# Column-group products in every second step from 20 to 30, full-array transposes of exponentials, and weight loads spread and issued ahead of the far writes

## The chip, the cores and the metric

The kernel runs on one core of a Trainium2 chip. The metric is the device time of one execution in microseconds; the median of the runs counts. The engines are TensorE (PE), VectorE (DVE), ScalarE (ACT) and GpSimd (POOL); SyncE (SP) issues the transfers. Each engine works through its own instructions in program order and waits on semaphores for the others.

## The reference

Three stages follow one another on the same tokens (4 batches, 8 heads, 576 positions, head size 64: 2304 tokens of 512 numbers). The first is causal attention with a decay. The other two, with names shortened:

```python
# stage 2: dense layer, 512 -> 2048 -> 512
h = x @ w_in
g = h * (1 / (1 + exp(-h)))
x = g @ w_out
# stage 3: soft mixture of 8 experts with 4 slots each (32 slots)
logits = x @ phi
d = softmax of logits over the tokens          # for each slot
slot_input = d.T @ x                           # 32 x 512, by experts
slot_out = relu(slot_input @ w1) @ w2          # each expert its own w1, w2
c = softmax of logits over the slots           # for each token
return c @ slot_out
```

## The kernel before

Attention takes the first 200 us or so, then the weights of stage 2 are prepared. Stage 2 and the sums of stage 3 run in 36 **steps**, numbered k from 0 to 35. Each belongs to a chunk c of 256 tokens (nine chunks, 0 to 8) and a group fg of 512 hidden numbers (four groups). From step 16 on a chunk's four groups follow one another: step 16 is (4,0), step 20 (5,0), step 24 (6,0), step 28 (7,0). A step has 24 products `h` (L594 to L596; two halves t of 128 tokens, 12 products each, f32 split into parts), and each half ends in ScalarE's tanh (`g_tanh`, L608) and VectorE's product (`g_mul`, L615), which give `gt`: tokens on partitions.

The work of stage 3 is put between the steps. Because the logits are linear, stage 2's second product is not made for each token: `W'` (`WP`, w_out times phi) turns g straight into logits. That needs g with hidden numbers on partitions, `gr`. There are two ways from gt to gr:
- `g_tr`, locally: eight transposes on TensorE over the full array (`gtp`, L658) and two copies on ScalarE (L659) into a buffer of the pool `w0` with the tag "t", which has two buffers;
- the "far" way: `blocks` has VectorE transpose blocks of 32 (`gb`, L667) and writes them to the chip's memory (`far`, L670), and `placed` reads them back in four transfers (`gr<-far`, L676). Before step 25 gb lies in a page of its own; from step 25 on (`own` false) it lies in a buffer of tag "t", as g_tr's result does.

`g_lp` then makes the logits of one (c,fg): products into four column groups of 32 columns (`lp`, L685), four side by side. When a chunk has its four groups, `chunk_soft` takes its logits (`sl`, L774) to exponentials, `chunk_w` transposes these (`etp`, L801) and makes the weights of both softmaxes, and `chunk_acc` adds the chunk's share to the slot sums (`pp`, L825, column groups again; accumulated by VectorE, L832). lp, pp and etp are not full-array products of 128 columns; h, gtp and sl are.

The order is written by hand in the functions at the end: after the h products of step k, `stacked(k)` does what is due of lp and pp and calls `place(k)`, which reads far tiles back; `square(k)` does transposes (g_tr by `turn_next`, chunk_w) and `turn_far`, which sends new far tiles out; `halfway(k)` stands between the two halves of a step. A list `flying` holds the (c,fg) that are on their way to g_lp.

The expert weights w1, w2 and the prepared w_out come in **units** of 512 KB (`load_unit`, L442, L448, L450) into free pages; `ROOM` says how many units may have been asked for by which step. All these transfers are issued by SyncE, in program order, in one queue.

Of the kernel before, what the change touches and what calls it, by code (L numbers as in the profile page):

```python
# [24 lines left out]
NPAGES = 25  # L25
NW = 8
STEPS = (17, 25, 30)
RATE = 1.5
CAPS = ((0, 12), (5, 6))
LAG = 1  # L30
ROOM = ((18, 5), (20, 6), (21, 7), (22, 10), (24, 11), (25, 12), (26, 17), (28, 19), (30, 23), (32, 29), (33, 32), (34, 35), (35, 42), (36, 45))
PARTS = ((0, 256, {}), (256, 128, {0: 1, 3: 2, 5: 2, 7: 2}), (384, 128, {1: 3, 3: 2, 5: 2, 7: 1}))
RING_A, RING_B, RING_T = "014", "235", "b"

# [2 lines left out]
def tile_attention_moe_softmoe(ctx: ExitStack, tc: tile.TileContext, qk, vr, f, wcat, phi, w1, w2, out):  # L37
    nc = tc.nc
# [6 lines left out]
    NCH = 9  # L45
# [13 lines left out]
    mo = {}  # L59

    def bank(ring, shape, name):
        tags = RINGS[ring]
        turn[ring] += 1
        ch = tags[turn[ring] % len(tags)]
        return ps.tile(shape, F32, name=name, tag=("av" if ch in "ab" else "b") + ch, bufs=1)

    ident = keep.tile([128, 128], F32, name="ident")
# [356 lines left out]
    def page(shape, name, dtype=F32):  # L424
        sl = FREE.pop(0)
        return sl[0].tile(shape, dtype, name=name, tag=sl[1], bufs=1), sl
# [293 lines left out]
    sm = {}  # L720

    def arena(a, **parts):
        at = 0
        for name, shape in parts.items():
            n = int(np.prod(shape))
            v = a[:, at:at + n]
            sm[name] = v.rearrange("p (a b) -> p a b", b=shape[1]) if len(shape) == 2 else v
            at += n
        assert at <= a.shape[1]
# [10 lines left out]
        arena(page([128, 1024], "arena")[0], WP=(2 * 8, 32), acc=(512,))  # L740

    def arena_b():
        arena(page([128, 1024], "arena")[0], sel=(128,), phi=(4, 32), wt=(2, 32), cw=(2 * NCH, 32), selz=(32,),
              mc=(1,), cm=(2, 1), cs=(2, 1), nm0=(1,), nm1=(1,), zc=(1,), sc0=(1,), sc1=(1,), z=(1,))
        nc.sync.dma_start(out=sm["phi"], in_=phi)
        for j in range(4):
            nc.vector.tensor_copy(sm["sel"][:, 32 * j:32 * j + 32], sm["rep"])
# [44 lines left out]
        scale()  # L792

    def chunk_w(c):
        e, wt, z, cm = sm["e"], sm["wt"], sm["z"], sm["cm"]
        cw = sm["cw"][:, 2 * c:2 * c + 2]
        tp = bank("g", [128, 2, 64], "etp")
        last = c == NCH - 1
        for t in range(2):
            n = 32 if last else 64  # L800
            nc.tensor.transpose(tp[:, t, 0:n], e[0:n, 128 * t:128 * t + 128], ident[0:n, 0:n])  # L801
        nc.vector.tensor_copy(wt, tp[:, :, 0:32])
        if c == 0:
            nc.vector.tensor_copy(z, sm["zc"])
        else:
            nc.vector.scalar_tensor_tensor(z, z, sm[f"scale{c}"], sm["zc"], op0=ALU.mult, op1=ALU.add)

        def weights():
            if last:
                for t in range(2):  # L810
                    nc.tensor.transpose(tp[:, t, 32:64], sm["ls"][32:64, 128 * t:128 * t + 128], ident[32:64, 32:64])
            tl = tp[:, :, 32:64]
            nc.vector.tensor_reduce(cm, tl, axis=AX.X, op=ALU.max)
            nc.vector.tensor_tensor(cw, tl, cm.to_broadcast([128, 2, 32]), ALU.subtract)
            nc.scalar.activation(cw, cw, AF.Exp)

        sm["weights"] = weights

    def chunk_acc(c):
        acc = sm["acc"]  # L820
        pp = bank("g", [128, 512], "pp")
        gt = [GT.pop((c, j)) for j in range(4)]
        for t in range(2):
            for j in range(4):
                nc.tensor.matmul(pp[32 * j:32 * j + 32], lhsT=sm["wt"][:, t], rhs=gt[j][:, t], start=(t == 0),  # L825
                                 stop=(t == 1))
        if c == 0:
            nc.vector.tensor_copy(acc, pp)
        else:
            n = 512 if c < NCH - 1 else 256  # L830
            for x in range(0, 512, n):
                nc.vector.scalar_tensor_tensor(acc[:, x:x + n], acc[:, x:x + n], sm[f"scale{c}"], pp[:, x:x + n],  # L832
                                               op0=ALU.mult, op1=ALU.add)
        release(*(GS.pop((c, j)) for j in range(4)))
# [197 lines left out]
    with tc.manual_schedule():  # L1032
# [66 lines left out]
            return 2 * fg + 1 in made and (c < 2 or c - 2 in read)  # L1099

        def turn_next(k):
            for f in rows[:3]:
                if turns[0] and born.get(f, 99) < int(k) and ready(*f) and f not in FAR:
                    turns[0] -= 1
                    turns[1] = k
                    rows.remove(f)
                    flying.append((k, *f))
                    g_tr(*f)
                    return
# [16 lines left out]
        def place(k):  # L1126
# [3 lines left out]
            for f in list(rows):  # L1130
                if f in FAR and born[f] < k and f[0] - rows[0][0] < 2 and ready(*f) and turns[0]:
# [2 lines left out]
                    flying.append((k, *f))  # L1134
                    placed(*f)

        def turn_soft():
            if soft:
                chunk_soft(soft[0])
                exps.append(soft.pop(0))  # L1140
                if soft:
                    chunk_ls(soft[0])

        def halfway(k):
            if STEPS[0] < k < STEPS[2]:
                turn_next(k - 0.5)
            turn_soft()

        def stacked(k):
            for f in sorted(flying, key=lambda f: f[1:]):  # L1150
                c, fg = f[1:]
                if f[0] < k:
                    flying.remove(f)
                    g_lp(c, fg)
                if SUMMED.get(c) == 4 and f not in flying:
                    if not soft:
                        chunk_ls(c)
                    soft.append(c)
            place(k)
            if acc and acc[0][0] < k:  # L1160
                chunk_acc(acc.pop(0)[1])
            if stage[0] is not None:
                w_prime_b(stage[0])

        def square(k):
            if stage[1] is not None:
                w_prime_c(stage[1])
            stage[1], was = stage[0], len(rows)
            stage[0] = mo["wp"].pop(0)[1] if mo["wp"] and mo["wp"][0][0] < k - bool(CQ) else None
            if stage[0] is not None:  # L1170
                w_prime_a(stage[0])
            else:
                turn_next(k)
            if exps:
                chunk_w(exps[0])
                chunk_cw(exps[0])
                acc.append((k, exps.pop(0)))
            turn_next(k)
            if k >= (NCH - 1) * 4:
                turn_soft()  # L1180
            if stage[0] is None and not STEPS[0] <= k < STEPS[2]:
                turn_next(k)
            turn_far(k)
            if stage[1] is not None and len(rows) < was:
                w_prime_c(stage[1])
                stage[1] = None

        conv_ops(OPS)
        for k, (c, fg) in enumerate(steps):
# [61 lines left out]
            elif fg != 2:  # L1251
                stacked(k + 0.5)
                if fg == 1:
                    square(k + 0.5)
            mo["umax"] = max([0] + [n for at, n in ROOM if k + 1 >= at])
            pump()
        assert not (soft or exps or acc) and rows == [(NCH - 1, 3)] and not mo["wp"], (soft, exps, acc, rows, mo["wp"])
        end()
        tail()
# [53 lines left out]
```

## Time and profile before

| | us |
|---|---|
| median of three runs | 536.07 (534.09 to 536.73) |
| profiled execution | 534.51 |
| its span, first to last instruction | 532.8 |
| TensorE busy (matmuls) | 506.1, 95% |
| TensorE loading weights, beside the matmuls | 373.7, 70% |
| VectorE busy | 338.1, 63% |
| ScalarE busy | 295.9, 56% |
| GpSimd busy | 212.8, 40% |

The span is what the profile covers; the execution's time is 1.7 us longer. In the rows a product's own duration overlaps with that of the next, since matmuls are pipelined: what a product costs is read from its start to the start of the next row. `x16` in a row joins 16 records that followed one another; each lp of one (c,fg) has eight records, a pp sixteen. In the stretch 310 to 444, which holds most of the changed steps, TensorE is busy 130.17 of 134 us. The granted clock of TensorE is 0.995 of full speed over the span.

The h products of step k end, and what stands behind them begins, at: step 22 at 359.28 us, 23 at 367.61, 24 at 375.08, 25 at 384.88, 27 at 403.58.

### The profile page before, as it was taken

How to read it: one execution, taken by the hardware profiler on the slowest of the kernel's cores; microseconds unless marked ns; L12 is line 12 of the kernel's file. 1: busy time of each engine (PE TensorE's matmuls, PEld its weight loads, DVE VectorE, ACT ScalarE, POOL GpSimd, SP SyncE). 2: the span in 40 equal slices, each digit the busy share in tenths (PEclk: the TensorE clock that was granted, in tenths of full speed). 3: DMA queues.
4: the chain of work that ended last, by engine and by line, in shares of the span. 5: the costliest groups of instructions: out<-in, count | busy, mean ns of one | idle time of the engine just before them, and what ended most of it. 6: DMA issues, size and time to landing. Idle time of an engine off the chain costs nothing.

```text
span 532.8 us, 11447 instructions
## 1 busy us (share of the span) xinstructions
PE 506.1 (95%) x4219; PEld 373.7 (70%) x4219; DVE 338.1 (63%) x896; ACT 295.9 (56%) x587; POOL 212.8 (40%) x237
## 2 busy tenths in 40 slices
PE   8899999999999999899999999999998999999994
PEld 4687887787777787587777777667675667674563
DVE  6766777677788389999989633655654431435033
ACT  8798889888886676557646554223421333331022
POOL 9777788888887304447466300000000000013000
PEclk9999999999999999999999999999999999999998
DMA  5727755665653387212431109699698818668998
GB/s 145 225 68 209 199 167 173 177 194 156 147 174 88 111 334 277 111 41 79 159 119 61 59 27 329 198 262 275 219 340 213 282 51 338 246 234 337 409 405 304
DMA packets 44108, 105.81 MB, mean 199 GB/s; under 512 B 8180, under 2 KB 17172, under 8 KB 44052
## 3 DMA queue, kind: packets, MB, share of 16 engines
q1 hardware_dynamic: 44052, 105.08, 60.3%
q8 instruction: 33, 0.54, 0.4%
q14 instruction: 23, 0.19, 0.1%
HBM read 82.58 MB, written 17.52 MB: 188 GB/s over the span
## 4 chain that ended last, share of the span: by engine, by line
PE 61%; DMA 12%; DVE 10%; ACT 7%; POOL 4%; issue 3%; SPq 2%; DVEq 0%; POOLq 0%; ACTq 0%
PE h L594 8%; PE h L596 8%; PE h L595 8%; PE av L304 4%; PE st L247 3%; PE gtp L658 3%; PE mx L201 3%; PE rs L288 3%; PE st L249 3%; PE lp L685 3%; PE so L959 3%; DMA gr<-far 3%; PE h L897 3%; DMA QA<-mr 3%; DMA far<-gb 2%
## 5 line engine op out<-in xcount | busy, mean ns | idle before, releaser
L594 PE MATMUL h<-w,xh 128*128 128x512 f32 x280 | 115.4, 412 | 3.7 <-DVE gt L615 3.7
L596 PE MATMUL h<-w,xh 128*128 128x512 f32 x280 | 110.5, 395 | 0.0
L595 PE MATMUL h<-w,xl 128*128 128x512 f32 x280 | 110.2, 394 | 0.0
L615 DVE SCALAR_TENSOR_TENSOR gt<-gt,h 128x512 f32<-128x512 f32 x70 | 46.9, 681 | 59.9 <-ACT gt L608 59.7
L608 ACT ACTIVATE gt<-h 128x512 f32<-128x512 f32 x70 | 41.4, 594 | 77.6 <-PE h L596 65.7
L253 ACT ACTIVATE E<-st 128x256 f32<-128x256 f32 (+4 forms) x160 | 63.5, 432 | 12.7 <-PE st L249 9.8
L207 DVE CUSTOM_DVE_ANT_0 junk<-mx,mask 128x64 bf16<-128x64 f32 (+3 forms) x128 | 50.0, 414 | 31.6 <-PE mx L201 30.8
L757 POOL COPY arena<-arena 128x128 f32<-128x128 f32 x4 | 1.1, 294 | 171.7 <-ACT gt L608 156.7
L594 PEld LDWEIGHTS h<-w,xh 128*128 128x128 f32 x280 | 52.6, 188 | 20.5 <-DVE gt L615 6.4
L596 PEld LDWEIGHTS h<-w,xh 128*128 128x128 f32 x280 | 52.6, 188 | 12.4
L247 PE MATMUL st<-QA,KA 128*128 128x256 f32 (+2 forms) x192 | 55.4, 300 | 5.3 <-DMA QA<-mr 2.9
L595 PEld LDWEIGHTS h<-w,xl 128*128 128x128 f32 x280 | 52.7, 188 | 10.7
L201 PE MATMUL mx<-KA,QA 127*128 127x64 f32 (+2 forms) x192 | 50.1, 327 | 2.0 <-DVE mr L222 1.0
L249 PE MATMUL st<-QB,KB 128*128 128x256 f32 (+2 forms) x192 | 51.6, 294 | 0.0
L270 POOL TENSOR_SCALAR_AFFINE_SELECT E<-E 128x256 f32<-128x256 f32 (+1 forms) x96 | 41.1, 444 | 26.1 <-ACT E L253 25.0
L304 PE MATMUL av<-E,VF 128*64 128x320 f32 (+4 forms) x448 | 50.8, 364 | 0.0
L179 POOL TENSOR_TENSOR QB<-qk,QA 64x576 fp32r<-64x576 f32 x30 | 42.8, 1428 | 2.3
L177 POOL TENSOR_TENSOR KB<-qk,KB 64x576 fp32r<-64x576 f32 x30 | 42.4, 1434 | 1.7 <-ACT KB L171 0.6
L304 PEld LDWEIGHTS av<-E,VF 128*64 128x64 f32 x448 | 29.5, 136 | 17.8 <-POOL E L270 0.3
L524 POOL TENSOR_TENSOR raw<-raw 128x512 f32<-128x512 f32 x16 | 26.9, 1681 | 37.1 <-ACT raw L513 30.0
L247 PEld LDWEIGHTS st<-QA,KA 128*128 128x128 f32 x192 | 34.6, 180 | 9.7 <-ACT E L253 7.1
L201 PEld LDWEIGHTS mx<-KA,QA 127*128 127x128 f32 x192 | 32.8, 189 | 6.1 <-DVE Mt L207 1.7
(170 smaller groups left out, 881.1 us busy)
## 6 DMA issues: line engine op xcount, KB each, us to landing
unit<-in_w_dram SPq DMA_DIRECT2D x64, 512.0 KB
raw<-in_w_dram SPq DMA_DIRECT2D x32, 512.0 KB
far<-gb SPq DMA_DIRECT2D x16, 512.0 KB
gr<-far SPq DMA_DIRECT2D x64, 128.0 KB
qk<-in_qk_dram SPq DMA_DIRECT2D x14, 576.0 KB
VF<-in_v_dram SPq DMA_DIRECT2D x16, 320.0 KB
RB<-R SPq DMA_DIRECT2D x32, 144.0 KB
WO<-wt SPq DMA_DIRECT2D x8, 512.0 KB
```

Of the source, the lines that this page charges most:

```text
L177: eng.tensor_tensor(KB.of(p)[0:64, h], src[64:128], KB.of(p)[64:128, h], ALU.subtract)
L179: eng.tensor_tensor(QB.of(p)[64:128, h], src[0:64], QA[p % 3][0:64, h, 64:640], ALU.subtract)
L201: nc.tensor.matmul(t[:, 0:w], lhsT=qa[0:127, h, 128 * blk:128 * blk + 128], rhs=ka[0:127, h, k0:k0 + w], start=True, stop=True)
L207: nc.vector.tensor_tensor_reduce(out=junk[:, 0:w], in0=t[:, 0:w], in1=mask[:, 448 - w:448], scale=1.0, scalar=Mx[p][:, h] if j == 5 else - ...
L247: nc.tensor.matmul(t[0:m, o:o + n], lhsT=ka[:, h, k0:k0 + m], rhs=qa[:, h, 64 + q0:64 + q1], start=True, stop=False)
L249: nc.tensor.matmul(t[0:m, o:o + n], lhsT=kb_[:, h, k0:k0 + m], rhs=qb[:, h, q0:q1], start=False, stop=True)
L253: nc.scalar.activation(e[0:m], t[0:m, 0:o], AF.Exp, scale=0.125)
L304: nc.tensor.matmul(AVP[p][x][64 * h:64 * h + 64, o0:o0 + n], lhsT=VF[p % 2][:, kb, h], rhs=E[2 * p + h][kb][:, c:c + n], start=kb == 0, st ...
L594: nc.tensor.matmul(o, lhsT=xh[:, d, tok], rhs=w[:, 0], start=(d == 0), stop=False)
L595: nc.tensor.matmul(o, lhsT=xl[:, d, tok], rhs=w[:, 0], start=False, stop=False)
L596: nc.tensor.matmul(o, lhsT=xh[:, d, tok], rhs=w[:, 1], start=False, stop=(d == 3))
L615: nc.vector.scalar_tensor_tensor(g, g, 1.0, h[:, n * j:n * j + n], op0=ALU.add, op1=ALU.mult)
```

## The change

Six things are changed in the steps 17 to 31:
- in the even steps of `APART` `stacked` only reads far tiles back; their lp and pp are made in the next odd step, together with that step's own;
- the transposes of exponentials (`etp`) take the full array: 128 rows instead of 64 (32 for the last chunk), into a buffer twice as wide;
- `wt`, the transposed exponentials, has two places, so that two chunks can stand side by side, since pp of one chunk may now come after the etp of the next;
- `turn_next` turns nothing locally in step 26 and while two local results are waiting;
- the units that a step loads (`rooms`) are issued within `square`, ahead of `turn_far`, in steps 17 to 30; before, they came at the end of the step, behind it;
- `ROOM` spreads the units over the steps: before, five at step 17, 1, 1, 3, 1, 1, 5, 2, 4 at steps 19, 20, 21, 23, 24, 25, 27, 29 and 6 at step 31; now 1, 2, 2, 3, 3, 3, 2, 3, 2 at steps 18, 21, 23, 25, 26, 27, 28, 29, 30 and 8 at step 31. By the end of step 31 both have 29.

```diff
+APART = (20, 22, 24, 26, 28, 30)
+ALONE = (26,)
...
-ROOM = ((18, 5), (20, 6), (21, 7), (22, 10), (24, 11), (25, 12), (26, 17), (28, 19), (30, 23), (32, 29), (33, 32), (34, 35), (35, 42), (36, 45))
+ROOM = ((19, 1), (22, 3), (24, 5), (26, 8), (27, 11), (28, 14), (29, 16), (30, 19), (31, 21), (32, 29), (33, 32), (34, 35), (35, 42), (36, 45))
...
     def arena_b():
-        arena(page([128, 1024], "arena")[0], sel=(128,), phi=(4, 32), wt=(2, 32), cw=(2 * NCH, 32), selz=(32,),
+        arena(page([128, 1024], "arena")[0], sel=(128,), phi=(4, 32), wt=(4, 32), cw=(2 * NCH, 32), selz=(32,),
               mc=(1,), cm=(2, 1), cs=(2, 1), nm0=(1,), nm1=(1,), zc=(1,), sc0=(1,), sc1=(1,), z=(1,))
+        sm["wt"] = sm["wt"].rearrange("p (c t) s -> p c t s", c=2)
...
     def chunk_w(c):
-        e, wt, z, cm = sm["e"], sm["wt"], sm["z"], sm["cm"]
+        e, wt, z, cm = sm["e"], sm["wt"][:, c % 2], sm["z"], sm["cm"]
         cw = sm["cw"][:, 2 * c:2 * c + 2]
-        tp = bank("g", [128, 2, 64], "etp")
         last = c == NCH - 1
+        tp = bank("g", [128, 4, 128], "etp")
         for t in range(2):
-            n = 32 if last else 64
-            nc.tensor.transpose(tp[:, t, 0:n], e[0:n, 128 * t:128 * t + 128], ident[0:n, 0:n])
-        nc.vector.tensor_copy(wt, tp[:, :, 0:32])
+            nc.tensor.transpose(tp[:, t], e[:, 128 * t:128 * t + 128], ident)
+        nc.vector.tensor_copy(wt, tp[:, 0:2, 0:32])
...
                 for t in range(2):
-                    nc.tensor.transpose(tp[:, t, 32:64], sm["ls"][32:64, 128 * t:128 * t + 128], ident[32:64, 32:64])
-            tl = tp[:, :, 32:64]
+                    nc.tensor.transpose(tp[:, 2 + t], sm["ls"][:, 128 * t:128 * t + 128], ident)
+            tl = tp[:, 2 * last:2 * last + 2, 32:64]
...
@@ -822,7 +824,7 @@
         gt = [GT.pop((c, j)) for j in range(4)]
         for t in range(2):
             for j in range(4):
-                nc.tensor.matmul(pp[32 * j:32 * j + 32], lhsT=sm["wt"][:, t], rhs=gt[j][:, t], start=(t == 0),
+                nc.tensor.matmul(pp[32 * j:32 * j + 32], lhsT=sm["wt"][:, c % 2, t], rhs=gt[j][:, t], start=(t == 0),
...
         def turn_next(k):
+            if k in ALONE or sum(f[1:] not in GRS for f in flying) == 2:
+                return
...
+        def rooms(k):
+            mo["umax"] = max([0] + [n for at, n in ROOM if k + 1 >= at])
+            pump()
...
+        def chunk_exps(k):
+            if exps:
+                chunk_w(exps[0])
+                chunk_cw(exps[0])
+                acc.append((k, exps.pop(0)))
+
         def stacked(k):
+            if k in APART:
+                place(k)
+                return
+            if k - 1 in APART:
+                chunk_exps(k - 0.5)
+                if len(acc) > 1:
+                    chunk_acc(acc.pop(0)[1])
...
-            if exps:
-                chunk_w(exps[0])
-                chunk_cw(exps[0])
-                acc.append((k, exps.pop(0)))
+            chunk_exps(k)
             turn_next(k)
...
+            if STEPS[0] <= k < 31:
+                rooms(k)
             turn_far(k)
...
-            mo["umax"] = max([0] + [n for at, n in ROOM if k + 1 >= at])
-            pump()
+            rooms(k)
```

**Where it moves instructions: TensorE.** Line numbers of the changed kernel are two or three higher. The rows are the work between the h products (left out at "..."), from the end of step 24 to the end of step 26 in the kernel before (lp and pp of step 24, lp and pp of step 25, sl, then step 26):

```order
L685 MATMUL lp<-gr,arena 32x256 x8
L825 MATMUL pp<-gt,arena 32x512 x8
L658 MATMUL gtp<-ident,gt 128x128 x8
L801 MATMUL etp<-ident,small 128x64 x2
...
L685 MATMUL lp<-gr,arena 32x256 x8
L825 MATMUL pp<-gt,arena 32x512 x8
...
L774 MATMUL sl<-small,arena 128x256
...
L685 MATMUL lp<-gr,arena 32x256 x8
L658 MATMUL gtp<-ident,gt 128x128 x8
L801 MATMUL etp<-ident,small 128x64 x2
```

In the change, from the end of step 24 (gtp and etp), over the sum product in step 25 and the end of step 25 (from etp to the second pp), to step 26 (sl, then etp) and step 27 (gtp in its middle, lp at its end):

```order
L660 MATMUL gtp<-ident,gt 128x128 x8
L803 MATMUL etp<-ident,small 128x128 x2
...
L777 MATMUL sl<-small,arena 128x256
...
L803 MATMUL etp<-ident,small 128x128 x2
L827 MATMUL pp<-gt,arena 32x512 x8
L687 MATMUL lp<-gr,arena 32x256 x16
L827 MATMUL pp<-gt,arena 32x512 x8
...
L660 MATMUL gtp<-ident,gt 128x128 x8
...
L687 MATMUL lp<-gr,arena 32x256 x16
```

Steps 24 and 26 have lost their lp and pp; step 25 has four lp between two pp, and step 27 four lp where before it had two.

**SyncE.** The transfers of the same stretch before, from the two far writes of step 24 to those of step 26; the numbers tell tiles apart:

```order
L670 DMA far_4937<-gb_4935 128x1024
L670 DMA far_4941<-gb_4939 128x1024
L448 DMA unit_4943<-in_w1_dram 128x1024
L676 DMA gr_4996<-far_4937 32x4x256 x4
L676 DMA gr_5001<-far_4941 32x4x256 x4
L670 DMA far_5018<-gb_5016 128x1024
L448 DMA unit_5020<-in_w1_dram 128x1024
...
L448 DMA unit_5028<-in_w1_dram 128x1024
L676 DMA gr_5076<-far_5018 32x4x256 x4
L670 DMA far_5108<-gb_5106 128x1024
L670 DMA far_5112<-gb_5110 128x1024
```

And in the change, from the reads of step 25 to the far writes of step 26:

```order
L678 DMA gr_4964<-far_4870 32x4x256 x4
L678 DMA gr_4969<-far_4874 32x4x256 x4
L444 DMA unit_4984<-WO5_4188 128x1024
L444 DMA unit_4986<-WO6_4261 128x1024
L444 DMA unit_4988<-WO7_4344 128x1024
L672 DMA far_4992<-gb_4990 128x1024
L678 DMA gr_5032<-far_4992 32x4x256 x4
L450 DMA unit_5049<-in_w1_dram 128x1024
L450 DMA unit_5051<-in_w1_dram 128x1024
L450 DMA unit_5053<-in_w1_dram 128x1024
L672 DMA far_5057<-gb_5055 128x1024
L672 DMA far_5061<-gb_5059 128x1024
```

Five units stood behind the one far write of step 25; in the change three stand ahead of it, and three more ahead of the two of step 26. far_4992 belongs to (5,2), far_5057 to (6,0).

**ScalarE.** With what each instruction waits for, at the two copies of the local turn after step 26 in the kernel before (tanh, the copies, the weights' exponential):

```order
L608 ACTIVATE gt_5043<-h_5053 128x512 [waits PE_49]
L659 ACTIVATE gr_5081<-gtp_5082 128x512 [waits PE_49,Activation_49]
L659 ACTIVATE gr_5081<-gtp_5088 128x512 [waits PE_49]
L815 ACTIVATE arena_3167<-arena_3167 128x64 [waits DVE_49]
```

And in the change, where g_tr of (5,3) stands in the middle of step 27:

```order
L817 ACTIVATE arena_3167<-arena_3167 128x64 [waits DVE_49]
L610 ACTIVATE gt_5076<-h_5063 128x512 [waits DMAHW1_49,DMAHW7_49,DMAHW0_49,PE_49]
L661 ACTIVATE gr_5079<-gtp_5080 128x512 [waits DMAHW4_49,DVE_49,PE_49]
L661 ACTIVATE gr_5079<-gtp_5086 128x512 [waits PE_49]
L610 ACTIVATE gt_5076<-h_5092 128x512 [waits PE_49]
```

The copy's first row has two waits that it did not have, for VectorE and for a transfer counted on DMAHW4; far_5057<-gb_5055 counts there.

## Rows read from the trace of the kernel before

**Rows 1.** The page's head.

```profile
span 532.8 us, 11447 instructions
```

**Rows 2.** Waits of TensorE from 315 to 470 us: total, times, longest.

```profile
PE lp L685 <- DMA gr<-far: 3.5, 4, 1.7
PE h L594 <- DVE gt L615: 0.2, 1, 0.2
```

**Rows 3.** Timeline of TensorE after step 24: start, duration, operation.

```profile
374.52 0.40 PE L595 MATMUL h<-w,xl 128*128 128x512 f32 x1
374.75 0.40 PE L596 MATMUL h<-w,xh 128*128 128x512 f32 x1
375.08 1.07 PE L685 MATMUL lp<-gr,arena 128*32 128x256 f32 x16
375.97 1.90 PE L825 MATMUL pp<-gt,arena 128*32 128x512 f32 x16
377.80 1.09 PE L658 MATMUL gtp<-ident,gt 128*128 128x128 f32 x8
378.83 0.33 PE L801 MATMUL etp<-ident,small 64*128 64x64 f32 x2
379.09 0.50 PE L594 MATMUL h<-w,xh 128*128 128x512 f32 x1
```

**Rows 4.** Timeline of TensorE after steps 22 and 23; in brackets idle time before.

```profile
359.28 1.07 PE L685 MATMUL lp<-gr,arena 128*32 128x256 f32 x16 [1.12 <-DMA gr<-far]
360.28 1.09 PE L658 MATMUL gtp<-ident,gt 128*128 128x128 f32 x8
361.13 0.48 PE L594 MATMUL h<-w,xh 128*128 128x512 f32 x1
361.45 0.40 PE L595 MATMUL h<-w,xl 128*128 128x512 f32 x1
...
368.61 0.33 PE L801 MATMUL etp<-ident,small 64*128 64x64 f32 x2
368.88 0.50 PE L594 MATMUL h<-w,xh 128*128 128x512 f32 x1
```

**Rows 5.** Timeline of TensorE, the first lp after steps 25 and 27.

```profile
384.88 1.07 PE L685 MATMUL lp<-gr,arena 128*32 128x256 f32 x16
...
403.58 1.07 PE L685 MATMUL lp<-gr,arena 128*32 128x256 f32 x16 [1.66 <-DMA gr<-far]
```

**Rows 6.** Timeline of SyncE's issues, steps 24 to 26: start, time spent issuing, count.

```profile
382.38 1.47 SPq L670 DMA_DIRECT2D far<-gb  x2
383.90 0.46 SPq L448 DMA_DIRECT2D unit<-in_w_dram  x1
385.42 3.64 SPq L676 DMA_DIRECT2D gr<-far  x8
389.75 0.34 SPq L670 DMA_DIRECT2D far<-gb  x1
390.13 2.74 SPq L448 DMA_DIRECT2D unit<-in_w_dram  x5
394.49 1.75 SPq L676 DMA_DIRECT2D gr<-far  x4
```

**Rows 7.** Timeline of VectorE after steps 24 and 27.

```profile
379.20 0.23 DVE L802 COPY arena<-etp 128x64 f32<-128x64 f32 x1 [0.48 <-PE etp L801]
...
381.11 2.37 DVE L667 STREAM_TRANSPOSE gb<-gt 128x1024 f32<-128x1024 f32 x2
...
404.72 1.25 DVE L667 STREAM_TRANSPOSE gb<-gt 128x1024 f32<-128x1024 f32 x1 [5.42 <-DMA far<-gb]
```

**Rows 8.** Timeline of ScalarE, the copies of one local turn.

```profile
378.50 1.09 ACT L659 ACTIVATE gr<-gtp 128x512 f32<-128x512 f32 x2 [2.71 <-PE gtp L658]
```

**Rows 9.** Windows: stretch, us, busy time of engines, TensorE's clock, transfer share, GB/s.

```profile
396.00:400.00 4.00, 4.00 (x19) 3.21 (x19) 2.65 (x9) 1.49 (x4) 0.00 (x0) 1.00 1.02 408
489.00:533.00 44.00, 36.88 (x682) 22.74 (x674) 10.62 (x24) 6.23 (x14) 2.23 (x3) 0.94 0.96 375
```

## The prediction

> **What bounds the kernel now.** The page comes first. TensorE is busy 506.1 of 532.8 us, so everything else counts only as far as TensorE waits for it or has fewer instructions to run [rows 1]. Second, the waits of TensorE over 315 to 470, which holds steps 18 to 35: lp waits four times for the transfer gr<-far, 3.5 us together, and h once for VectorE, 0.2 [rows 2]. So at most 3.7 us of waiting can go there; the rest must come from shorter TensorE work. Third, the timeline of TensorE, read by the distance from one start to the next: between h products 0.23 [rows 3], at the changes of kind of product more [rows 3, 4]. Fourth, the timelines of SyncE, VectorE and ScalarE, since the change moves transfers, and the windows, for how full the transfers are: a full share (1.02, 408 GB/s) in 396 to 400, where the kernel now waits most [rows 9].
>
> **Fewer runs of column-group products.** Entry: the last h to the first lp takes 0.33 where h to h takes 0.23, 0.10 more [rows 3]. Exit: a run of two lp lasts 0.89 where pp follows, in the same column groups [rows 3], and 1.00 where a full-array transpose follows, 0.11 more [rows 4]. So a run costs 0.21 over its products. In before there is one after each of steps 20 to 31, twelve; in the change after the odd ones, six: 6 x 0.21 = 1.3 us less (1.0 if one of the six keeps it).
>
> **Full-array transposes of exponentials.** The gtp run lasts 0.85 before h [rows 4] but 1.03 before the half-height etp, and etp 0.26: 0.18 + 0.26 = 0.44 for etp there [rows 3]. After lp it takes 0.27 [rows 4]. Of the eight chunks 0 to 7 four stand each way: 4 x 0.44 + 4 x 0.27 = 2.8. After the change etp is two more transposes of the gtp kind, 2 of 8 of 0.85, 0.21 each, 1.7 together: 1.1 us less. (Where it stands alone between h products it pays up to 0.09 more, the 0.32 of the first h after gtp less 0.23 [rows 4]; 0.9 is the lower bound.)
>
> **One local turn less.** By the order, local transposes after step 18 go from twelve runs to eleven, and the far round trips from 16 to 17: 0.85 less on TensorE [rows 4]. The extra round trip is one more far write and four reads back on a queue that is full in places; it is in the waits below.
>
> TensorE's work therefore falls by 1.3 + 1.1 + 0.85 = 3.2 us. No stage is left whose cover hides that saving: TensorE itself is the bound. The doubled wt, the page order and the accumulations are VectorE work of the same count, beside h.
>
> **The waits.** All four old waits for gr, at steps 22, 23, 27 and 28 (1.12, 0.25, 1.66, 0.5), can go: the products that need gr come up to a step later, at 23 and then at 27 and 29. 3.7 us less. What is late next? I followed each chain through the new order. The tight one is at step 27, time zero being the end of step 25's h (384.88 in before [rows 5]).
>
> TensorE: step 25's tail is etp 0.3, pp 1.83, four lp 2 x 0.89, pp 1.83 = 5.7; step 26's h 5.8 (379.09 to 384.88 [rows 3, 5]) and sl 0.4 (half of the 0.89, by its columns) = 11.9; step 27: etp 0.2, half its h 2.8, gtp 0.95, the other half 2.9 = 18.7; three lp 1.3: the last, lp(5,3), is due at 20.1.
>
> Its input is turned locally in the middle of step 27: the two ScalarE copies gr<-gtp write a buffer of tag "t", which the change's order shows waiting for DMAHW4, the transfer far(6,0)<-gb. In before the same copy waits only for TensorE and ScalarE; there VectorE's transpose waited for such a transfer instead, 5.42 us [rows 7], beside other work. ScalarE is in order: behind the copies stands step 27's second tanh.
>
> The chain: VectorE can write gb(6,0) after etp at 11.9 + 0.3, its 1.9 of weight work (379.20 to 381.11) and 1.2 for a transpose (half of 2.37) [rows 7]: 15.3. SyncE: eight gr parts start at about 2.5 (0.54 after the end of h in before, 385.42 - 384.88 [rows 5, 6]; between 0.5 and 5, since pages come free only as the tail runs) and take 3.6 [rows 6], so to 6.1; three units 1.4 (0.46 to 0.55 each by 2.74 for five [rows 6]): 7.5; far(5,2) issued at 7.6. How long far takes with three units directly ahead of it no row shows. Below: 3.0, from far's issue at 382.38 to the gr that waits for it at 385.42 [rows 6]; with eight gr parts ahead 4.7 (389.75 to 394.49 [rows 6]); above: 4.7 and three units in full, each 512 KB at the 408 GB/s of the full share, 1.28 [rows 9]: 8.5. I take 6.5, midway, so 14.1. gr(5,2) issues 1.75 [rows 6], 15.9; three units, 17.3; far(6,0) at 17.3. For it I take 5.4, the wait of VectorE for the same kind of transfer in this stretch [rows 7]: 22.7. Two copies 1.09 [rows 8]: 23.8, against 20.1: a stall of 3.7; with some knock-on on the tanh, **4.0**. Its bounds: 0, if far(6,0) goes out as soon as gb is there (15.3 + 3.0 + 1.1 = 19.4, before 20.1); and 8.8, if each unit ahead adds its full 1.28 and the gr start late.
>
> Step 25 (lp(4,0), whose far stands behind two units): 0 to 2, as one step less of time lies between its far and its lp; taken 0.7, by the small old waits of 0.25 and 0.5. Step 29, alike with more room: 0 to 1, taken 0.3. New waits 5.0 together.
>
> The Trainium skill, "DMA: Bandwidth & Descriptors", section "Queues, rings and completion order", bears on the upper bound: on each of the 16 engines descriptors are consumed in ring order, so a far write behind three units starts only after their share. By that rule the wait would be near the 8.8 end and the sum near 537.4 for the profiled run; rival B below is that case. The trace leans that way (3.0 with little ahead, 4.7 with eight parts ahead), but no row has units directly ahead of a far.
>
> After step 31 the two orders agree, and by then both have the same count of units loaded; the tail's TensorE is busy 36.88 of 44 us beside a transfer share of 0.96 [rows 9]. It moves rigidly.
>
> **Sum.** 534.51 (the profiled run: span 532.8 and 1.7 around it) - 3.2 - 3.7 + 5.0 = 532.6. The median of the runs is 1.56 over that run, which lies low within 534.09 to 536.73; I add 1.2: 533.8.
>
> **The rivals.** 0.5% is 2.7 us, about what a measurement of this kernel can tell from no change; so 533.4 and 538.7 are the bounds.
> - A: the far round trips keep pace. far takes 3.0 to 4.5 even behind units, and the stall at step 27 is 0 to 2. For it: transfers of 512 KB spread over all engines, and units asked for earlier are done earlier. Against: 396 to 400 is full already. New waits 0 to 4.2 give 528.8 to 533; 530.8 in the middle (new waits 2).
> - B, the other side: the units ahead of far in the one queue cost their full time. Step 27 waits 8.8, step 25 2.0, step 29 1.0: 11.8, so 540.6. It is slower from new waits of 9.6 on. For it: one queue in program order, and ScalarE's copy, tanh and then VectorE's product chained behind it. Against: 8.8 needs the late gr start as well.
> - C: the change of kind costs nothing when runs are joined, the price sitting in the products' own start, and etp keeps its time: TensorE saves only 0.85, and with new waits 5.0 the time is 536.2, no change.
>
> **How the numbers follow.** The forecast gets 0.42: the chain's middle values, each from the nearest row. A gets 0.33, B 0.17, C 0.08. The forecast at 533.8 lies just inside the lower bound; 0.07 of its chance falls beyond it. Faster: 0.33 + 0.07 = 0.40. Slower: 0.15 of B. Same: 0.45. The range leaves out most of B and the lowest of A: 529.6 to 538.4; the forecast's own is 532 to 536.
>
> **What would show it.** Six runs of column-group products between steps 20 and 31, a run's lp at 0.44 each and etp at 0.2 to 0.3 behind h: then the 3.2 is right. No wait of lp for gr at steps 22, 23, 28: then the 3.7 is right. In the changed kernel's waits, lp waiting some 4 us for ScalarE's gr near 400, and ScalarE's gr waiting there for DMA far<-gb: then the step 27 chain is right. No such wait means A; over 8, or waits of lp for gr of over 2 us at several odd steps, means B. lp runs that last longer per product when joined, or long first h products in even steps, mean C. The forecast would be wrong, too, if VectorE's transposes gb, which stand in its order ahead of the products of gt, held back the h that wait for their banks.

## The result, and the profile after

| | before | after |
|---|---|---|
| median of eight runs | 536.08 us | 539.86 us |
| range of the runs | 534.09 to 538.89 | 537.63 to 543.91 |
| ratio, 95% interval | | 1.0075 (1.0046 to 1.0105) |
| profiled execution, its span | 534.51, 532.8 | 539.53, 537.8 |

The change makes the kernel 0.75% slower, outside the range that was given. The page's head of the changed kernel, and its row of TensorE's granted clock in 40 slices:

```profile
span 537.8 us, 11447 instructions
PEclk9999999999999999899999999999996999999999
```

The waits of TensorE in 310 to 480, which answer to [rows 2] (total, times, longest):

```profile
PE lp L687 <- ACT gr L661: 6.4, 1, 6.4
PE lp L687 <- DMA gr<-far: 2.4, 2, 2.2
PE etp L803 <- DVE small L785: 0.8, 1, 0.8
```

The old waits at steps 22, 23 and 28 are gone; 8.6 us of the new ones stand at one place, the end of step 27. Its timeline on TensorE (start, duration, operation, idle time before):

```profile
398.91 1.07 PE L687 MATMUL lp<-gr,arena 128*32 128x256 f32 x16
402.17 1.03 PE L687 MATMUL lp<-gr,arena 128*32 128x256 f32 x8 [2.19 <-DMA gr<-far]
409.62 1.13 PE L687 MATMUL lp<-gr,arena 128*32 128x256 f32 x6 [6.42 <-ACT gr L661]
410.48 1.07 PE L827 MATMUL pp<-gt,arena 128*32 128x512 f32 x2
410.54 0.64 PE L687 MATMUL lp<-gr,arena 128*32 128x256 f32 x2
410.96 2.67 PE L827 MATMUL pp<-gt,arena 128*32 128x512 f32 x14
413.56 0.50 PE L596 MATMUL h<-w,xh 128*128 128x512 f32 x1
```

lp(5,2) waits for its transfer, then lp(5,3) for ScalarE. ScalarE's copy for it waits in turn, with the releaser in brackets:

```profile
408.97 1.08 ACT L661 ACTIVATE gr<-gtp 128x512 f32<-128x512 f32 x2 [13.01 <-DMA far<-gb]
```

SyncE's issues before that, which answer to [rows 6] (start, time spent issuing, count):

```profile
370.36 0.38 SPq L672 DMA_DIRECT2D far<-gb  x1
377.95 1.74 SPq L678 DMA_DIRECT2D gr<-far  x4
379.79 0.85 SPq L672 DMA_DIRECT2D far<-gb  x2
383.36 4.81 SPq L678 DMA_DIRECT2D gr<-far  x8
388.26 1.32 SPq L444 DMA_DIRECT2D unit<-WO  x3
389.68 0.38 SPq L672 DMA_DIRECT2D far<-gb  x1
397.39 1.74 SPq L678 DMA_DIRECT2D gr<-far  x4
399.24 1.32 SPq L450 DMA_DIRECT2D unit<-in_w_dram  x3
400.61 1.36 SPq L672 DMA_DIRECT2D far<-gb  x2
408.93 4.93 SPq L678 DMA_DIRECT2D gr<-far  x8
```

The first three rows belong to steps 23 and 24. A gr read is issued when its far write has landed; where SyncE's wait for that write ends last, the time from one issue to the other is the landing. far(5,2), issued at 389.68 behind three units, landed at 397.4, after 7.7 us; far(6,0), at 400.61 behind three more, at 408.9, after 8.3. SyncE itself stands still meanwhile, and what is behind the waiting read in its order too. And the clock (windows: stretch, us, busy time of the engines, granted clock, transfer share, GB/s):

```profile
400.00:402.00 2.00, 0.00 (x0) 0.00 (x0) 0.00 (x0) 0.00 (x0) 0.00 (x0) 1.00 1.06 261
402.00:404.00 2.00, 1.03 (x8) 0.16 (x8) 0.00 (x0) 0.00 (x0) 0.00 (x0) 0.57 0.97 303
...
410.00:412.00 2.00, 2.00 (x16) 0.98 (x16) 0.69 (x1) 0.93 (x3) 0.00 (x0) 0.50 0.74 220
412.00:414.00 2.00, 2.00 (x16) 0.70 (x8) 0.32 (x1) 0.00 (x0) 0.00 (x0) 0.87 0.59 160
```

TensorE stood idle from 400 on; its clock fell to 0.5, that is from 2.4 to 1.2 GHz, and stayed there until after 412. lp(5,3) and pp run at that level.

The saving on TensorE is there as well. Timeline after steps 20 and 21, to be held against [rows 3, 4]:

```profile
340.98 1.04 PE L660 MATMUL gtp<-ident,gt 128*128 128x128 f32 x8
341.85 0.38 PE L803 MATMUL etp<-ident,small 128*128 128x128 f32 x2
...
347.75 1.92 PE L827 MATMUL pp<-gt,arena 128*32 128x512 f32 x16
349.49 1.91 PE L687 MATMUL lp<-gr,arena 128*32 128x256 f32 x32
351.21 1.90 PE L827 MATMUL pp<-gt,arena 128*32 128x512 f32 x16
```

gtp to etp 0.87 instead of 1.03, etp to h 0.14 (h follows at 341.99) instead of 0.26; four lp in one run take 1.72, 0.43 each.

Where the 5.0 us between the two profiled runs lie: the first lp of step 18 starts at 324.29 before and 325.64 after, that of step 31 at 437.56 and 442.86. So **the stretch from step 18 to step 31**, which holds nearly all of the change, takes 113.27 before and 117.22 after, 3.95 more. The rest behind it takes 95.2 and 94.9. What stands ahead of step 18 is the same work of TensorE in all kernels here, but ended anywhere between 323.3 and 329.9 in the profiled runs; so this stretch is given below beside the ratios. Ratios are to the kernel before, with their 95% interval; a stretch is that of one profiled run.

### The profile page after: what moved, and what is told of

It is laid out like the page before. It is cut to its first block, busy times and chain, and to the rows that moved or that the text cites. A ratio compares the mean times of both kernels' runs of the same rounds, so it can differ in the third digit from the quotient of the medians.

```text
span 537.8 us, 11447 instructions
## 1 busy us (share of the span) xinstructions
PE 506.4 (94%) x4211; PEld 375.2 (70%) x4211; DVE 334.6 (62%) x897; ACT 294.5 (55%) x585; POOL 214.0 (40%) x237
## 4 chain that ended last, share of the span: by engine, by line
PE 71%; DVE 9%; DMA 9%; ACT 6%; issue 2%; POOL 1%; SPq 1%; DVEq 0%; ACTq 0%; POOLq 0%
PE h L596 9%; PE h L598 9%; PE h L597 9%; PE av L306 6%; PE mx L203 4%; PE st L249 4%; PE rs L290 4%; PE lp L687 3%; PE st L251 3%; PE gtp L660 3%; DMA far<-gb 3%; PE pp L827 3%; PE so L961 3%; PE h L899 3%; DMA QA<-mr 2%
## 5 line engine op out<-in xcount | busy, mean ns | idle before, releaser
L272 POOL TENSOR_SCALAR_AFFINE_SELECT E<-E 128x256 f32<-128x256 f32 (+1 forms) x96 | 43.6, 469 | 24.0 <-ACT E L255 22.6
L526 POOL TENSOR_TENSOR raw<-raw 128x512 f32<-128x512 f32 x16 | 25.5, 1592 | 38.6 <-ACT raw L515 31.5
L661 ACT ACTIVATE gr<-gtp 128x512 f32<-128x512 f32 x36 | 19.6, 597 | 31.8 <-PE gtp L660 18.8
```

The costliest lines, as they stand in the source:

```text
L272: nc.gpsimd.affine_select(out=e, in_=e, pattern=pattern, compare_op=ALU.is_ge, fill=0.0, base=0, channel_multiplier=-1)
```

## The experiments

My theory after the result: units ahead of far writes in SyncE's queue make the far writes land late, and the round trips of steps 25 to 27, one behind the other, make step 27 late. The rivals: only the shared buffer of ScalarE's copy is at fault; all transfers together are too much, whatever their order; the new order of products (APART) itself is at fault.

**Is it the shared buffer?** Two kernels remove that wait. The first gives the far tiles of steps 25 and 26 pages of their own (`STEPS[1]` is 25), the second turns (5,3) at the end of step 26:

```diff
-                        blocks(*f, k < STEPS[1])
+                        blocks(*f, k < 27)
```

> The changed kernel, but the far tiles of steps 25 and 26 are transposed into pages of their own instead of buffers of tag t, so that the local turn of (5,3) at step 27 no longer shares a buffer with a far write on its way. Theory (the stall at step 27 is ScalarE's copy waiting for far(6,0), and the slow far writes alone cost little else): the wait of lp for ScalarE's gr, 6.4 us, goes to under 0.5; lp's wait for gr<-far at step 27, 2.2, stays; the granted clock around 402 to 412 stays near 1.0 instead of 0.5, which gives back some 1.6 more; the ratio to the kernel before falls from 1.0075 to 0.990 to 0.996. Rival (far writes themselves are too slow, and the wait moves to the next lp that needs gr): the time stays at 1.004 or more, with a new wait of lp for gr of 4 us or more at step 29.

Ratio 1.0115 (1.0080 to 1.0151), the stretch 120.70.

```diff
-ALONE = (26,)
+ALONE = ()
```

> The changed kernel without the rule that nothing is turned locally in step 26: (5,3) is turned at the end of step 26, ahead of the far writes of (6,0) and (6,1), and its buffer comes from an earlier far write; transfers stay as they are. Theory: ScalarE's copy waits for no far write that is on its way; the 6.4 at step 27 goes. In its place VectorE's transpose for (6,1) waits for lp(5,3), and the products of step 27's gt behind it: h waits 0 to 1.5 at step 28. lp's 2.2 for gr at step 27 stays. Ratio to before 0.990 to 0.997. Rival (the far writes are what is late): waits of 4 us or more elsewhere, ratio 1.003 or more.

Ratio 1.0130 (1.0083 to 1.0177), the stretch 120.64. TensorE's waits from 310 to 480, of the first kernel and then of the second:

```profile
PE lp L687 <- DMA gr<-far: 11.9, 3, 9.1
```

```profile
PE lp L687 <- DMA gr<-far: 9.9, 3, 7.0
```

ScalarE's wait is gone in both, as expected, and nothing is won: lp waits for gr instead, 9.1 us at step 29 in the first kernel. Its far write there, issued at 416.42, landed at 424.8, again over 8 us and again behind three units. The rival of both expectations holds. The shared buffer was only the first place at which late far writes were felt.

**Is it the order of units and far writes?**

```diff
-            if STEPS[0] <= k < 31:
-                rooms(k)
             turn_far(k)
```

> The changed kernel, but each step's units are issued behind its far writes, as in the kernel before; their number per step stays. Theory (a far write lands late because the units ahead of it in SyncE's queue go first): far(5,2) lands 3 to 5 us after its issue instead of 7.7, far(6,0) 3 to 5.5 instead of 8.3; the wait of lp for gr at step 27 goes, that for ScalarE's gr falls from 6.4 to under 2; ratio to before 0.988 to 0.996. Rival (the writes are slow because all transfers of the stretch are, wherever the units stand): both land after 7 us or more again, and the ratio stays at 1.004 or more.

Ratio 0.9939 (0.9907 to 0.9971), the stretch 114.56. SyncE from step 26's far writes on, and the waits of TensorE's lp:

```profile
395.53 1.46 SPq L672 DMA_DIRECT2D far<-gb  x2
397.10 2.02 SPq L450 DMA_DIRECT2D unit<-in_w_dram  x3
399.25 8.53 SPq L678 DMA_DIRECT2D gr<-far  x8
```

```profile
PE lp L687 <- DMA gr<-far: 5.0, 1, 5.0
PE lp L687 <- ACT gr L661: 0.6, 1, 0.6
```

The far writes land after 3.1 (step 25) and at most 3.7 us (step 26), and step 27 is nearly free. But units now stand ahead of the gr reads; in this profile those end later, and lp waits 5.0 at step 29: order decides which transfer is late, and the bytes in these steps remain. The profiled run took 536.57, near the slowest of its twelve, and their median is 532.51, 7 us below the changed kernel; its 5.0 and its stretch need not hold for the others.

**Is it the queue or the amount?** Units of steps 17 to 30 issued by GpSimd:

```diff
-            nc.sync.dma_start(out=t, in_=WOH[f2])
+            (nc.gpsimd if 17 <= mo["k"] < 31 else nc.sync).dma_start(out=t, in_=WOH[f2])
```

(the two other transfers of `load_unit` alike).

> The changed kernel with the units of steps 17 to 30 issued by GpSimd, whose queue is another one, instead of SyncE; the order around them stays. Theory A (a far write lands late because units stand ahead of it in the same queue): far(5,2) and far(6,0) land 3 to 5 us after their issue, not 7.7 and 8.3; the stall at step 27 falls from 8.6 to under 3; ratio 0.988 to 0.997. Theory B (what is late is late because all transfers of the stretch together ask for more than they get; whose queue it is doesn't matter): far writes and gr reads take as long as before the move, waits of lp and of ScalarE's copy 7 us or more together over steps 25 to 29, ratio 1.003 or more.

Ratio 1.0044 (1.0018 to 1.0069), the stretch 114.04. far(5,2) landed after 4.9 us (391.12 to 396.01), but far(6,0), with units of the other queue beside it, after 7.9 (399.65 to 407.50); ScalarE's copy still waited 8.6 us and lp 3.6 for it, 2.5 for gr. Another queue helps in part, between the two theories, and nearer to that of the amount. It is no clean test of the queue alone: far(5,2) was issued 3.4 us behind the last of its step's units (387.74), while two units were issued behind far(6,0) (402.69 and 405.44) before it landed.

Units put off from steps 25 to 27, order as in the change; only `ROOM` differs, given here as the count of units by the end of a step:

```
changed kernel    18: 1, 21: 3, 23: 5, 25: 8, 26: 11, 27: 14, 28: 16, 29: 19, 30: 21, 31: 29
this run          18: 1, 21: 6, 28: 8, 29: 13, 30: 21, 31: 29
```

> The changed kernel with the same order, but no units in steps 25 to 27: six by step 21, 8 by step 28, 13 by 29, 21 by 30 and 29 by 31, as in the changed kernel from there. Both theories of the queue and of the total take the stall at step 27 away (no unit ahead, less to move): far(5,2) and far(6,0) land within 3 to 5 us, waits of lp for gr and ScalarE's gr under 2 together at 27, 2 or less at 29. The sum without them is 534.5 - 3.2 - 3.7 + 1 to 3 = 528.6 to 530.6 for a run like the profiled one of before: ratio 0.988 to 0.994. Rival (the units that come later are missed at the end): h of the last stage waits for units after 489 us, ratio 0.998 or more.

Ratio 0.9944 (0.9916 to 0.9972), the stretch 110.83. Steps 25 to 29 are free of waits for transfers; the one that is left (3.1) stands at step 23, behind the five units that step 21 now has. The same with the units behind the far writes:

> As the run with deferred units, and units issued behind the far writes as well. If the place in the queue matters beside the amount: the far writes of steps 28 and 29, which have units in their step, land 2 us earlier than with the units ahead, and the ratio is 0.002 to 0.006 lower than there. If the amount alone matters: the two agree within 0.002.

Ratio 0.9957 (0.9935 to 0.9979), the stretch 112.90: no difference that the intervals tell. With step 21 as in the change (18: 1, 21: 3, 23: 5, 28: 8, then as above):

> As the run with deferred units, but step 21 takes two units and step 23 two, as in the changed kernel, instead of five at step 21; none in steps 24 to 27. There lp waited 3.1 us for gr at step 23, after five units in step 21. Theory: that wait goes too, and all waits of lp in steps 21 to 29 stay under 1 together: 3 us less than with deferred units, ratio 0.986 to 0.992. Rival (the wait at step 23 has another cause): it stays, ratio 0.993 to 0.997.

Ratio 0.9918 (0.9888 to 0.9948), the stretch 106.06. lp waits for nothing in 315 to 480.

**What does one unit cost?** One in each of steps 25 to 27, ahead of the far writes:

> As the run before it in this batch, but one unit in each of steps 25, 26 and 27, ahead of the far writes: a dose between none and the changed kernel's three. Theory: each unit ahead adds 1.0 to 1.6 us to the landing of the far write behind it (3.0 to 3.4 without, 7.7 and 8.3 with three); far(5,2) and far(6,0) land after 4.2 to 5 us, the stall at step 27 is 0 to 1.5, ratio 0.988 to 0.995. Rival (a step from none to any): landing after 6 us or more, ratio 0.998 or more.

Ratio 0.9905 (0.9876 to 0.9935), the stretch 110.37. SyncE's far writes and the reads that wait for them:

```profile
386.94 0.38 SPq L672 DMA_DIRECT2D far<-gb  x1
393.28 1.75 SPq L678 DMA_DIRECT2D gr<-far  x4
...
395.60 0.85 SPq L672 DMA_DIRECT2D far<-gb  x2
400.93 4.53 SPq L678 DMA_DIRECT2D gr<-far  x8
```

far(5,2) landed after 6.3 and far(6,0) after 5.3 us, where 3.8 and 2.7 were measured in the run without these units, and lp waited 3.7 at steps 25 and 27. Both theories missed: a unit costs more than its 1.3 at the full rate, and the ratio is low all the same. In the stretch this kernel is 4 us behind the one without units there, by the medians it isn't, and one profile each doesn't settle it. The same dose behind the far writes:

> One unit in each of steps 25 to 27 as in the run with the dose of one, but issued behind the step's far writes. There the far writes of (5,2) and (6,0) landed 6.3 and 5.3 us after their issue, against 3.8 and 2.7 without units, more than the 1.3 us of a unit at 408 GB/s. Theory 1 (a unit delays what stands behind it in the queue, and nothing else): both land within 4 us again, no wait of lp at step 27; from lp of step 18 to lp of step 31 106 to 108 us, as without units in these steps. Theory 2 (the unit costs its share of the full stretch wherever it stands): lp waits 2 us or more for gr or for ScalarE's copy in steps 27 to 29, and that stretch is 109 us or more.

Ratio 0.9882 (0.9858 to 0.9906), median 529.32 us, the lowest here; the stretch 106.07. SyncE's issues in steps 25 and 26, and TensorE's waits in 310 to 480:

```profile
387.74 0.34 SPq L672 DMA_DIRECT2D far<-gb  x1
388.18 0.38 SPq L444 DMA_DIRECT2D unit<-WO  x1
390.70 1.74 SPq L678 DMA_DIRECT2D gr<-far  x4
396.25 1.46 SPq L672 DMA_DIRECT2D far<-gb  x2
397.77 0.45 SPq L444 DMA_DIRECT2D unit<-WO  x1
398.97 4.57 SPq L678 DMA_DIRECT2D gr<-far  x8
```

```profile
PE etp L803 <- DVE small L785: 0.8, 1, 0.8
PE etp L803 <- ACT small L783: 0.4, 1, 0.4
```

With one unit behind each, the far writes land after 3.0 and 2.7 us, and no lp waits. By these profiles the place in the queue is what counts at this dose; the ratios of the two kernels overlap in their intervals and do not tell them apart. Three units in step 26 alone, ahead (18: 1, 21: 3, 23: 5, 26: 8, 28: 9, 29: 13):

> Three units in step 26, ahead of its two far writes, none in 25 and 27: the price of the place. Theory: far(5,2) lands within 4 us and lp's wait for gr at step 27 is 0; far(6,0) lands 6 to 8.5 us after issue, ScalarE's copy and lp(5,3) wait 2 to 5; from lp of step 18 to that of step 31 108 to 112 us; ratio 0.990 to 0.997. If step 25's three units are what makes step 27 late: no wait at step 27 here, the stretch 106 to 107.

Ratio 0.9952 (0.9929 to 0.9975), the stretch 110.17. far(5,2) landed after 3.1 us; far(6,0) after 5.1, less than the 6 expected; it was issued 2.3 us behind the units' last issue, which may be why. lp(5,3) waited 2.0. So units of both steps made step 27 late: those of step 26 alone give 2.0 of the 8.6. The granted clock fell to 0.51 behind that wait, and lp and pp take 2.1 more over the stretch than in the kernel with one unit behind.

**Is it APART?**

```diff
-APART = (20, 22, 24, 26, 28, 30)
+APART = ()
```

> The changed kernel without APART: column-group products after each step again, twelve runs; the transposes of exponentials, the units ahead of the far writes and their spread over the steps stay as changed. Theory (the units cost, APART gains): lp needs its gr up to a step earlier, with far writes as late as in the changed kernel: lp waits for gr 8 us or more over steps 22 to 29, and twelve runs cost 1.3 more on TensorE: ratio 1.008 to 1.020. Rival (APART is what delays: tiles stay longer on their way, and transfers are bunched): waits under 5, ratio under 1.003.

Ratio 1.0155 (1.0123 to 1.0187), the stretch 124.05 (lp of step 31 at 448.54, of step 18 at 324.49). TensorE's waits:

```profile
PE lp L687 <- ACT gr L661: 6.5, 1, 6.5
PE lp L687 <- DMA gr<-far: 6.1, 4, 4.2
```

12.6 us of waits: with the units as changed, APART gains 0.8%. And the kernel before with its units of steps 25 and 27 put off to 29 and 30 (17: 5, 19: 6, 20: 7, 21: 10, 23: 11, 24: 12, 29: 18, 30: 23):

> A control: the kernel before, with its order of work, and its units of steps 25 and 27 put off to step 29 (12 by step 24, 18 by 29, 23 by 30, 29 by 31). Theory (what the deferral is worth and what APART is worth are two things): the wait of lp at step 27 (1.7) and the one at 28 (0.5) go, those at 22 and 23 stay: 2 to 3 us less, ratio 0.994 to 0.997, and the changed order with deferred units remains 2 to 4 us below it. Rival (all of the gain of deferred units is theirs, and APART gives nothing): the same ratio here as there, within 0.002.

Ratio 0.9967 (0.9948 to 0.9986), the stretch 111.19, lp's waits 1.5 instead of 3.5. Deferring gains 2 us in the old order. The new order without units in steps 24 to 27 stands another 5 below it in the stretch, and 2.6 by the ratios (0.9918).

**The clock.** Products without use in step 27, ahead of lp(5,2) and lp(5,3):

```diff
+                    if k == 27 and fg > 1:
+                        warm_up(8 if fg == 2 else 24)
                     g_lp(c, fg)
```

> The changed kernel with extra products in step 27 whose result is not used, 8 ahead of lp(5,2) and 24 ahead of lp(5,3), so that TensorE works while it waits (5.6 + 1.9 us at full clock, where the waits are 6.4 and 2.2). Theory (the granted clock falls because TensorE stands idle, and lp and pp behind the wait run at half of it): the clock in 402 to 414 stays at 1.0, lp(5,3) and pp take 2.3 us instead of 3.9, and the time is 1 to 2 us under that of the changed kernel: ratio 1.003 to 1.006 beside its 1.0075. Rival (the clock falls there for another reason, or filling delays lp): the clock falls all the same, and the ratio is 1.0075 or more.

Ratio 1.0063 (1.0036 to 1.0089), the stretch 117.23. The windows and the timeline:

```profile
406.00:408.00 2.00, 2.00 (x10) 1.59 (x10) 0.00 (x0) 0.00 (x0) 0.00 (x0) 1.00 1.00 404
...
412.00:414.00 2.00, 2.00 (x19) 0.75 (x12) 0.76 (x2) 0.38 (x1) 0.00 (x0) 1.00 0.85 223
```

```profile
410.99 0.90 PE L687 MATMUL lp<-gr,arena 128*32 128x256 f32 x6 [1.49 <-ACT gr L661]
411.59 0.62 PE L827 MATMUL pp<-gt,arena 128*32 128x512 f32 x2
411.72 0.39 PE L687 MATMUL lp<-gr,arena 128*32 128x256 f32 x2
411.93 1.89 PE L827 MATMUL pp<-gt,arena 128*32 128x512 f32 x14
413.75 0.51 PE L596 MATMUL h<-w,xh 128*128 128x512 f32 x1
```

The clock stays at 1.0, so it was the idle time that lowered it; lp(5,3) and pp take 2.76 (410.99 to 413.75) instead of 3.94. But the stretch is as long as without. lp of step 29 takes 2.88 instead of 1.75, since it waits 0.94 for gr in its middle, and step 29's second pp starts 102.5 us behind lp of step 18 in both profiles: what was gained at step 27 is lost to transfers that come no earlier. By the ratios it isn't settled; the intervals overlap.

**The transposes alone**, in the kernel before:

```diff
-            nc.tensor.transpose(tp[:, t, 0:n], e[0:n, 128 * t:128 * t + 128], ident[0:n, 0:n])
+            nc.tensor.transpose(tp[:, t], e[:, 128 * t:128 * t + 128], ident)
```

> The kernel before with one part of the change alone: the transposes of exponentials over the full array, all else as before. The term of the sum for it was 1.1 us (0.9 to 1.1) less. If it holds: gtp to etp 0.85 to 0.88 instead of 1.03, etp to h 0.14 behind gtp and 0.19 behind lp instead of 0.26; TensorE 1.1 to 1.6 us less over eight chunks; ratio 0.997 to 0.998, which the interval will hardly tell from 1. If the form of the transposes costs nothing: the intervals of TensorE's rows as in the kernel before.

Ratio 0.9994 (0.9972 to 1.0016): not to be told from 1, as expected. gtp to etp is 0.97 in the row looked at (378.48 to 379.45), between the two values; in that profile lp waited 0.9 longer for gr than in [rows 2], so what it saves alone is not read from its time. The rows tell it: over the stretch, start to start, gtp and etp take 7.5 us instead of 8.5, 1.0 less for seven chunks, where 1.1 was worked out for eight.

## Why the prediction was wrong

**What bounds the kernel; TensorE's savings: right.** The chain through far writes, reads and TensorE was the one that decided. Six runs, etp and the turn were to save 3.2, the old waits 3.7, 6.9 together. Where no lp waits (the two kernels with the stretch at 106.1) it is 113.27 - 106.06 = 7.2 shorter, with a new 0.8 of etp's wait in it: 8.0 shorter without that. Of this, 3.8 are the old waits, and 0.4 is one lp that the new order puts behind the end of the stretch; TensorE's work fell by the other 3.8, where 3.2 was worked out. By the ratios these two kernels are 4.4 and 6.3 us below the kernel before; for the first, 7.2 lies outside the interval, and one profile doesn't tell why. etp behind gtp saved 0.28 (1.03 + 0.26 to 0.87 + 0.14) where 0.23 was worked out, behind lp 0.08 where 0.06 was. Two figures of the working are off by a little: the four old waits for gr make 3.5, and the 3.7 holds the 0.2 of h as well, which went too; and by its own sum the change is slower from new waits of 9.9 on, not 9.6.

**The place of the new wait: right.** Step 27, lp(5,3), ScalarE's copy held by far(6,0), and gr(5,2) ahead of it.

**Its size: wrong, the step "I take 6.5, midway" and "For it I take 5.4".** From the end of step 25's h (379.13: etp's 379.93 less its 0.80 of idle) the terms were, and measured:

| | taken | measured |
|---|---|---|
| first gr read of step 25 starts | 2.5 | 4.2 |
| far(5,2) issued | 7.6 | 10.5 |
| its landing takes | 6.5 | 7.7 |
| far(6,0) issued | 17.3 | 21.5 |
| its landing takes | 5.4 | 8.3 |
| stall before lp(5,2) and lp(5,3) | 4.0 | 8.6 |

Every term erred to the same side. The start of the reads was wrong in its path: 2.5 was taken between bounds set by pages that come free. In the changed kernel the reads waited for the far write of step 24, issued at 379.79; that stood in SyncE's order behind the read at 377.95, which had waited 7.2 us for step 23's far write (370.36), issued right behind two units (369.41). So the chain began two steps earlier than the one that was worked out. An issue that is late makes all behind it in the queue late. The landings were mis-sized besides: 6.5 was a midpoint between rows, and 5.4 came from a far write (issued at 399.32 before) with no unit directly ahead of it. I had put middle values into a chain in which all depends on one queue.

The upper bound of the stall, 8.8, is nearly what came, and rival B, given 0.17, is the case that came: three units ahead of a far write cost most of their time, and the reads started late. That its 540.6 is so near the median of 539.86 is in part luck: its 2.0 and 1.0 at steps 25 and 29 were 0.16 and 0, and what is left out below stood in for them. The Trainium skill's rule that was set beside it ("DMA: Bandwidth & Descriptors", "Queues, rings and completion order", descriptors of one engine consumed in ring order) agrees with the runs: 3.0 and 2.7 us with a unit behind, 6.3 and 5.3 with it ahead, 7.7 and 8.3 with three. It gave the profiled run 537.4; it took 539.53. Ring order in one queue does not by itself give the 7.9 us that far(6,0) took with the units on GpSimd's queue.

**Left out: the slower products behind the stall, and etp.** Start to start over the stretch, idle time apart, lp and pp take 23.9 us, against 21.5 where no lp waits: 2.4 more. With the clock held at 1.0 (the run with products without use) they take 22.1, so some 1.7 of the 2.4 goes with the lowered clock, 1.2 of it on lp(5,3) and pp. And etp at step 25 waited 0.8 for VectorE's copy (L785) of the logits that it transposes beside the exponentials, which the new order puts right ahead of it. Step 25's price was taken as 0.7 by far writes; 0.16 was the gr wait there. Step 29's 0.3 was 0.

**The sum again**, for the stretch, with measured terms: 113.27 - 4.24 (TensorE's work, the displaced lp with it) - 3.76 (old waits) + 8.61 + 0.16 + 0.80 (new waits) + 2.37 (slower lp and pp) = 117.2, as measured. Rival A (round trips keep pace) became true only where the units were fewer or behind. Rival C, which left TensorE 0.85, is refuted by the 3.8.

## What to carry to other kernels

Count a transfer queue as an engine: a round trip through memory waits for what stands ahead of it in its queue (and here nearly as long, 7.9 against 8.3 us, for loads issued beside it from another queue), and several in a row add up before any engine shows a wait. Take bulk loads out of the steps in which short transfers are waited for, or issue them behind these; here the same order of TensorE's work was 0.75% slower or 1.2% faster than before by the place and the number of the loads alone. When another buffer removes a wait, look for the next place where the late transfer is needed, since it may cost as much there.

## What the runs showed of the hardware

A unit of 512 KB ahead of a far write delayed it by more than its bytes at the 408 GB/s of [rows 9] (1.3 us): by 2.5 us with one ahead (6.3 against 3.8, both issued some 0.5 us behind eight reads). The second pair (5.3 against 2.7) says less, since the 5.3 was issued 0.6 us behind four reads and the 2.7 3.0 us behind them. With three ahead the far writes of the changed kernel took 7.2 to 8.3 us; with three behind 3.1 and at most 3.7.

TensorE's clock fell from 1.0 to 0.5 behind a wait of 2.0 us (three units in step 26 alone) and one of 3.1 us (step 23 with five units in step 21), but stayed at 1.0 through a wait of 3.1 us in the run with one unit ahead, and of 1.66 in the kernel before. The length of the wait alone does not tell these cases apart.
